# Three norms ahead instead of two: where the rows for the second product's norms are loaded

## The chip, the cores and the metric

The kernel runs on one core of one Trainium2 chip. The metric is device time in microseconds (us) of one execution; of several executions the median is taken.

## The reference

Four sublayers in a row over `x` of 2048 x 512 float32; each adds its result to its input. Sublayers 0 and 2 are a Fourier mixing, 1 and 3 a gated feed-forward (F = 1792):

```python
def _A_ref(x, ...):                      # layers 0 and 2
    a = einsum("bsd,ed->bse", x, dft_hid_re)
    b = einsum("bsd,ed->bse", x, dft_hid_im)
    return einsum("ts,bse->bte", dft_seq_re, a) - einsum("ts,bse->bte", dft_seq_im, b)

def _B_ref(x, w_gate, w_up, w_down):     # layers 1 and 3
    return (gelu(x @ w_gate) * (x @ w_up)) @ w_down

x = x + _A_ref(layernorm(x), ...)
x = x + _B_ref(layernorm(x), ...)
x = x + _A_ref(layernorm(x), ...)
x = x + _B_ref(layernorm(x), ...)
```

## The kernel before

Each float32 operand is split into a high part (a rounded copy, made on ACT, line 151) and a low part (the rest, made on DVE, line 153), and each product of two tiles is three matmuls (high x high, high x low, low x high: lines 208, 209, 210, the helper `mm3`). The large products are computed by a Strassen-like scheme with seven block products, named A11, A12, S1 to S4 and A22. A matmul writes one of eight PSUM banks (`p`); ACT copies banks out (line 195, `copied`), seeds one bank from another (line 202, `seed`) and computes the GELU (line 1019, `activated`); DVE adds (line 188, `plus`).

SBUF holds 98 slots of 128 x 512 (`s`). The free ones stand in a list: `get` takes the first one and `put` adds at the end, so the k-th tile that is taken reuses the slot that was given back earliest. In some stages two wide tiles (`wide`, `xwide`) are lent out as further slots.

The feed-forward layers handle the 2048 rows in two halves, `w` = 0 and 1, each of two blocks of 512 rows. A half takes 14 steps, `up(n)`. Step n has seven products of six matmuls each over weight tiles `wb` (loaded two steps ahead by `piece_load`, line 1009, on SP's queue), and beside them six matmuls of the product with the third weight (tiles `wc`, line 327). `first(n)` starts the bank `chain[n]` with A11 and seeds a second bank from it; `second(n)` adds A12 there and applies the GELU; `u[n]` is the copy of `chain[n]` after S2, and S3 is added to the same bank afterwards.

The rows of a half are normalised before it starts. `block_steps(layer, w)` makes eight steps `norm(i)` for this, each over 128 rows. A step takes its rows in a mixed order, by `x_load_mixed` (line 245: four transfers of 32 rows each on SP's queue), then computes mean and variance on ACT (lines 564 and 566, with a power on POOL, lines 567 and 568), applies them on ACT (line 590), transposes on DVE (line 672) into a wide tile, and after four steps POOL stores that tile (line 675). What `norm(i)` loads is the subject here: the first step loads several rows at once, a later one a row that a later step uses.

For `w` = 0 the eight steps stand among the products of the mixing layer before, in the stages of its second and third output block (`chores_at`). There the first four read output block 0 and the last four output block 1, and rows are never loaded across that border: `end` is the end of the four. For `w` = 1 they stand in the list `slow` and are run one by one, every ninth product, while half 0 is computed. Steps 0 to 3 of half 1 read output block 2 and steps 4 to 7 (rows 12 to 15 of the sixteen) block 3, which the mixing layer writes at its very end (line 278, `x_out`).

The program is written in this order, but a scheduler then places each instruction on its engine by its own estimate of times. Each engine carries out its instructions strictly in the order in which they were placed: one that waits holds all behind it. That holds for SP's queue of transfers too.

Of the kernel before, what the change touches and what calls it, by code (L numbers as in the profile page):

```python
# [21 lines left out]
NT = TB // P  # L22
# [25 lines left out]
def fnet_geglu(ctx: ExitStack, tc: tile.TileContext, x_in, ws, wh, wgu, wdn, wdc, out):  # L48
# [113 lines left out]
    def split_slot(src):  # L162
        hi, lo = sb.get(F32R), sb.get(F32R)
        split(src, hi, lo)
        return hi, lo
# [16 lines left out]
    def minus(out, a, b):  # L182
        with behind("DVE"):
            nc.vector.tensor_tensor(out, a, b, op=ALU.subtract)  # L184
# [54 lines left out]
    def x_load_mixed(layer, i):  # L239

        g, n = divmod(i, NT)
        t = sb.get()
        for j in range(NT):
            r0 = j * P + n * 32
            nc.sync.dma_start(t[j * 32:(j + 1) * 32], xs[layer, g][r0:r0 + 32])
        return t
# [335 lines left out]
    def normed(layer, i, mixed=False):  # L582
        x = row_of(layer, i, mixed)
        z = sb.get()
        rstd, shift = known.pop((layer, i), None) or norm_terms(layer, i, x, z)
        if layer == 0 and i == 0:
            for h in half:
                nc.scalar.activation(z[:, h], x[:, h], AF.Identity, bias=shift, scale=rstd)
        else:
            nc.scalar.activation(z, x, AF.Identity, bias=shift, scale=rstd)  # L590
        sb.put(x)
        return z
# [61 lines left out]
    def block_steps(layer, w):  # L654

        zt, t, wide = {}, {}, {}
        turned = [dram.tile([P, NT * D], F32, name=f"t{layer}_{w}_{part}") for part in range(2)]

        def norm(i):

            def run():
                r0 = w * 2 * NT
                end = 2 * NT if w else i // NT * NT + NT
                for k in range(i if i == 0 or i + NT == end and not w else i + 2, min(i + 3, end)):
                    fresh["mixed", r0 + k] = x_load_mixed(layer, r0 + k)
                z = normed(layer, r0 + i, True)
                part, n = divmod(i, NT)
                if n == 0:
                    assert not sb.out("z")
                    wide[part] = tpool.tile([P, NT * D], F32, name="wide")  # L670
                to = wide[part].rearrange("p (b n t) -> p b n t", n=NT, t=32)
                nc.vector.transpose(to[:, :, n], z.rearrange("p (b t) -> p b t", t=32))
                sb.put(z)
                if n == NT - 1:
                    nc.gpsimd.dma_start(turned[part], wide.pop(part))
            return run

        def fetch(c):

            def run():  # L680
                for part in range(2):
                    v = zt[c, part] = sb.get()
                    for i in range(P // 32):
                        cols = turned[part][:, (c * 4 + i) * P:(c * 4 + i + 1) * P]
                        to = v[i * 32:(i + 1) * 32]
                        (nc.gpsimd if w == 0 else nc.sync).dma_start(
                            to.rearrange("p (j t) -> p j t", t=P), cols.rearrange("(j p) t -> p j t", p=32)
                        )
            return run

        def difference(a, b):
            v = sb.get()
            minus(v, a, b)
            return v

        def first(c):
            def run():
                v = t[f"B{1 + c // 2}1", c % 2] = zt.pop((c, 0))
                blocks[f"B{1 + c // 2}1", c % 2] = split_slot(v)
            return run  # L700

        def second(c):
            def run():
                v = zt.pop((c, 1))
                if c < 2:
                    t["B12", c] = v
                    t["T1", c] = difference(v, t["B11", c])
                    sb.put(t.pop(("B11", c)))
                else:
                    c0 = c - 2  # L710
                    t["T2", c0] = difference(v, t["T1", c0])
                    t["T3", c0] = difference(v, t["B12", c0])
                    sb.put(t.pop(("B12", c0)))
                    blocks["B22", c0] = split_slot(v)
                    sb.put(v)
            return run

        def fourth(c):
            def run():
                t["T4", c] = difference(t["B21", c], t["T2", c])  # L720
                sb.put(t.pop(("B21", c)))
            return run

        def divide(name, c):
            def run():
                blocks[name, c] = split_slot(t[name, c])
                sb.put(t.pop((name, c)))
            return run

        one = [norm(i) for i in range(2 * NT)]  # L730
        two = [fetch(c) for c in range(ND)] + [first(c) for c in range(ND)] + [second(c) for c in range(ND)]
        two += [fourth(c) for c in range(2)]
        two += [divide(name, c) for name in ("T2", "T3", "T1", "T4") for c in range(2)]
        return one, two
# [773 lines left out]
```

## Time and profile before

| what | value |
|---|---|
| time, median of 3 runs | 1611.77 us (1610.68 to 1614.64) |
| time of the profiled execution | 1611.43 us |
| span of the profiled execution, first to last instruction | 1609.7 us |
| mean granted TensorE clock | 0.998 |
| TensorE (PE) busy | 1597.4 us, 99% of the span |
| VectorE (DVE), ScalarE (ACT), GpSimd (POOL) busy | 70%, 55%, 17% |
| data moved | 419.14 MB, 260 GB/s on average |

In the rows of the profile `PE` is the matmul, `PEld` the weight load beside it, `SPq` the queue on which SP issues transfers. A group `p<-s,s` writes a bank from two slots. `[6.47 <-DMA s<-x]` behind a row says that the engine stood idle for 6.47 us before it, and what ended that. Times in a timeline are us from the start of the span. The profiled execution took 1.7 us more than its span.

### The profile page before, as it was taken

To read this page: it belongs to the slowest core of one execution; us is meant where nothing else is said; L and a number is where in the kernel's file an instruction comes from. 1 tells how busy PE (TensorE), PEld (TensorE's weight loads), DVE (VectorE), ACT (ScalarE), POOL (GpSimd) and SP (SyncE) were. 2 spreads that over 40 slices of the span, in tenths; PEclk is the share of its full clock that TensorE was granted. 3 is DMA by queue.
4 is the path that set the end of the run, shared out by engine and by line. 5 is a ranking of instruction groups with operands and counts; after the bars stand their busy time and mean duration, and the time that the engine had idled before them with its cause. 6 is when DMAs were issued, how large, how long until landed. Compare 5 with 4: busy or idle time off the path is not lost.

```text
span 1609.7 us, 22615 instructions
## 1 busy us (share of the span) xinstructions
PE 1597.4 (99%) x7008; PEld 1316.5 (82%) x7008; DVE 1132.5 (70%) x1958; ACT 885.1 (55%) x1711; POOL 271.7 (17%) x469
## 2 busy tenths in 40 slices
PE   9999999999999999999999999999998999999998
PEld 6888888888888888888788888888887888888887
DVE  7997878787699783456879877777744457744574
ACT  8955466654767554546566636465444545433460
POOL 4112121242556101000040001101310000000001
PEclk9999999999999999999999999999999999999999
DMA  9878887996999899755896776878999576895445
GB/s 358 294 262 301 297 312 258 344 323 207 338 350 317 275 357 289 230 170 181 273 306 200 250 256 219 305 235 291 251 312 266 165 216 193 309 307 166 125 150 157
DMA packets 238872, 419.14 MB, mean 260 GB/s; under 512 B 28512, under 2 KB 66656, under 8 KB 237728
## 3 DMA queue, kind: packets, MB, share of 16 engines
q1 hardware_dynamic: 214512, 336.16, 65.3%
q0 software_dynamic: 24240, 81.55, 14.3%
q8 instruction: 55, 0.90, 0.2%
q14 instruction: 65, 0.53, 0.1%
HBM read 341.31 MB, written 76.28 MB: 259 GB/s over the span
## 4 chain that ended last, share of the span: by engine, by line
PE 94%; DMA 3%; DVE 1%; ACT 1%; issue 0%; SPq 0%; POOL 0%; DVEq 0%; ACTq 0%; POOLq 0%
PE p L208 31%; PE p L209 31%; PE p L210 31%; DMA s<-x 1%; DMA xwide<-x 1%; DMA s<-wc 1%; PE p L809 1%; DMA begun<-wide 0%; DVE s L153 0%; DMA s<-wb 0%; DVE s L184 0%; DMA s<-begun 0%; DVE s L188 0%; ACT s L151 0%; SPq L1271 0%
## 5 line engine op out<-in xcount | busy, mean ns | idle before, releaser
L209 PE MATMUL p<-s,s 128*128 128x512 f32 x2320 | 900.4, 390 | 0.0
L210 PE MATMUL p<-s,s 128*128 128x512 f32 x2320 | 893.7, 389 | 0.0
L208 PE MATMUL p<-s,s 128*128 128x512 f32 x2320 | 867.2, 390 | 5.9 <-ACT s L1019 4.4
L153 DVE TENSOR_TENSOR s<-s,s 128x512 fp32r<-128x512 f32 (+1 forms) x809 | 507.6, 661 | 126.7 <-ACT s L151 110.4
L151 ACT ACTIVATE s<-s 128x512 fp32r<-128x512 f32 (+1 forms) x809 | 454.5, 607 | 239.2 <-DVE s L184 65.9
L208 PEld LDWEIGHTS p<-s,s 128*128 128x128 f32 x2320 | 436.0, 188 | 98.7 <-ACT s L1019 4.9
L209 PEld LDWEIGHTS p<-s,s 128*128 128x128 f32 x2320 | 436.1, 188 | 91.2 <-DVE s L153 1.0
L210 PEld LDWEIGHTS p<-s,s 128*128 128x128 f32 x2320 | 436.2, 188 | 90.7
L188 DVE TENSOR_TENSOR s<-s,p 128x512 f32<-128x512 f32 x188 | 127.2, 683 | 166.8 <-PE p L210 136.9
L184 DVE TENSOR_TENSOR s<-s,s 128x512 f32<-128x512 f32 (+1 forms) x374 | 222.8, 612 | 5.6 <-PE p L209 3.6
L195 ACT ACTIVATE s<-p 128x512 f32<-128x512 f32 x232 | 134.6, 594 | 123.2 <-PE p L210 119.7
L1019 ACT ACTIVATE s<-s 128x512 f32<-128x512 f32 x84 | 52.8, 629 | 60.2 <-DVE s L188 50.5
L567 POOL TENSOR_SCALAR rstd<-rstd 128x1 f32<-128x1 f32 x40 | 20.5, 512 | 363.3 <-ACT s L566 347.4
L153 DVE TENSOR_TENSOR s<-xwide,s 128x512 fp32r<-128x512 f32 x71 | 47.7, 678 | 33.5 <-ACT s L151 33.2
L313 POOL DMA_DIRECT2D wb<-s x84 | 46.6, 569 | 87.8 <-ACT s L151 67.6
L1033 DVE TENSOR_TENSOR s<-s,p 128x512 f32<-128x512 f32 x56 | 38.3, 684 | 32.3 <-PE p L210 29.6
L151 ACT ACTIVATE s<-xwide 128x512 fp32r<-128x512 f32 x71 | 43.0, 621 | 15.5 <-DVE xwide L184 6.6
L1019 ACT ACTIVATE s<-p 128x512 f32<-128x512 f32 x28 | 16.7, 597 | 63.3 <-PE p L210 59.8
L590 ACT ACTIVATE s<-s,shift,rstd 128x512 f32<-128x512 f32 x56 | 44.9, 811 | 10.9 <-DMA s<-x 4.9
L202 ACT ACTIVATE p<-p 128x512 f32<-128x512 f32 x56 | 32.8, 586 | 30.6 <-PE p L210 30.4
L191 DVE TENSOR_TENSOR s<-s,s 128x512 f32<-128x512 f32 (+1 forms) x68 | 40.6, 605 | 8.6 <-DMA s<-ws 6.7
L564 ACT ACTIVATE s<-s 128x512 f32<-128x512 f32 x33 | 20.7, 626 | 46.4 <-DMA s<-x 27.9
(100 smaller groups left out, 613.4 us busy)
## 6 DMA issues: line engine op xcount, KB each, us to landing
s<-ws SPq DMA_DIRECT2D x384, 256.0 KB, 4.9
s<-wb SPq DMA_DIRECT2D x294, 256.0 KB, 5.0
s<-wc SPq DMA_DIRECT2D x182, 256.0 KB, 4.4
s<-wh SPq DMA_DIRECT2D x116, 256.0 KB, 5.1
wb<-s POOLq DMA_DIRECT2D x98, 256.0 KB, 5.4
s<-x SPq DMA_DIRECT2D x59, 256.0 KB, 5.3
xwide<-ws SPq DMA_DIRECT2D x50, 256.0 KB, 4.6
wc<-s POOLq DMA_DIRECT2D x49, 256.0 KB, 5.6
```

Source lines behind the costliest of these rows:

```text
L151: newest["ACT"] = nc.scalar.activation(hi, src, AF.Copy)
L153: newest["DVE"] = nc.vector.tensor_tensor(lo, src, f32(hi), op=ALU.subtract)
L184: nc.vector.tensor_tensor(out, a, b, op=ALU.subtract)
L188: bank_read["DVE"] = nc.vector.tensor_tensor(out, a, b, op=ALU.add)
L191: nc.vector.tensor_tensor(out, a, b, op=ALU.add)
L195: bank_read["ACT"] = nc.scalar.activation(v, src, AF.Copy)
L208: nc.tensor.matmul(ps, ah, bh, start=start, stop=False, skip_group_check=True)
L209: nc.tensor.matmul(ps, ah, bl, start=False, stop=False, skip_group_check=True)
L210: nc.tensor.matmul(ps, al, bh, start=False, stop=stop, skip_group_check=True)
L313: nc.gpsimd.dma_start(a, f32(t))
L590: nc.scalar.activation(z, x, AF.Identity, bias=shift, scale=rstd)
L1019: nc.scalar.activation(t, g, AF.Gelu_apprx_tanh)
```

## The change

In `norm(i)` the range of rows to load moves by one. Before, step 0 loads the rows of steps 0, 1 and 2, and step i the row of step i + 2. After, step 0 loads those of steps 0 to 3, and step i the row of step i + 3. For `w` = 0 this means that all four rows of a block are loaded in the first of its four steps. The number of loads and every computation stay the same; one slot more is held between the earlier load and its former place.

```diff
             def run():
                 r0 = w * 2 * NT
                 end = 2 * NT if w else i // NT * NT + NT
-                for k in range(i if i == 0 or i + NT == end and not w else i + 2, min(i + 3, end)):
+                for k in range(i if i == 0 or i + NT == end and not w else i + 3, min(i + 4, end)):
                     fresh["mixed", r0 + k] = x_load_mixed(layer, r0 + k)
                 z = normed(layer, r0 + i, True)
```

## The prediction

> **What bounds the kernel now.** I read the page first, then the waits of PE, then the stages around each of them.
>
> ```profile
> span 1609.7 us, 22615 instructions
> ...
> PE 1597.4 (99%) x7008; PEld 1316.5 (82%) x7008; DVE 1132.5 (70%) x1958; ACT 885.1 (55%) x1711; POOL 271.7 (17%) x469
> ```
>
> PE is the bound, at 99%. A load can only pay where PE stands still. The waits of PE alone:
>
> ```profile
> PE p L208 <- ACT s L1019: 4.4, 1, 4.4
> PE p L1418 <- POOL ident masks.py:199: 1.4, 1, 1.4
> PE p L208 <- DMA s<-wc: 1.1, 1, 1.1
> PE p L208 <- ACT s L195: 0.3, 1, 0.3
> ```
>
> That is the whole list. One wait is large, and it happens once. The timeline of PE shows its place, early in layer 3, half 0 (step n = 2 of 14):
>
> ```profile
> 1219.82 0.39 PE L208 MATMUL p<-s,s 128*128 128x512 f32 x1
> 1220.05 0.39 PE L209 MATMUL p<-s,s 128*128 128x512 f32 x1
> 1220.27 0.61 PE L210 MATMUL p<-s,s 128*128 128x512 f32 x2
> 1225.32 0.80 PE L208 MATMUL p<-s,s 128*128 128x512 f32 x1 [4.44 <-ACT s L1019]
> 1225.91 0.63 PE L209 MATMUL p<-s,s 128*128 128x512 f32 x1
> ...
> 1229.75 0.63 PE L209 MATMUL p<-s,s 128*128 128x512 f32 x1
> 1230.18 0.54 PE L210 MATMUL p<-s,s 128*128 128x512 f32 x1
> 1230.56 0.39 PE L208 MATMUL p<-s,s 128*128 128x512 f32 x1
> ```
>
> Ahead of the stop a matmul starts every 0.227 us (1219.82, 1220.05, 1220.27). Behind it one starts every 0.43 us (1229.75, 1230.18). The granted clock tells why:
>
> ```profile
> 763.00:768.00 5.00, 3.88 (x18) 2.90 (x17) 5.00 (x10) 2.88 (x6) 0.00 (x0) 1.00 1.05 390
> 1220.50:1225.30 4.80, 0.39 (x2) 0.00 (x0) 0.71 (x1) 2.51 (x7) 0.05 (x1) 0.83 1.02 245
> 1225.30:1230.50 5.20, 5.18 (x12) 4.16 (x13) 1.53 (x3) 4.27 (x9) 1.30 (x3) 0.50 1.02 370
> ```
>
> The third column from the end is the clock: 0.50 for 5.2 us after this stop, 1.00 around the shorter one near 766 us. The whole price: 13 starts from 1220.50 (the second of the pair of 1220.27) to 1230.56 take 10.06 us, and at 0.227 us they would take 2.95. **This place costs 7.1 us**, 0.44% of the time.
>
> What held PE is told by ACT, SP and the chain of waits, in this order:
>
> ```profile
> 1216.02 0.29 ACT L569 ACTIVATE shift<-mean,rstd 128x1 f32<-128x1 f32 x1 [0.24 <-POOL rstd L568]
> 1222.79 0.63 ACT L564 ACTIVATE s<-s 128x512 f32<-128x512 f32 x1 [6.47 <-DMA s<-x]
> ...
> 1223.42 0.80 ACT L590 ACTIVATE s<-s,shift,rstd 128x512 f32<-128x512 f32 x1
> 1224.12 0.57 ACT L195 ACTIVATE s<-p 128x512 f32<-128x512 f32 x1
> ...
> 1224.69 0.58 ACT L1019 ACTIVATE s<-p 128x512 f32<-128x512 f32 x1
> ```
>
> ```profile
> 1204.77 1.22 SPq L327 DMA_DIRECT2D s<-wc  x1
> 1206.83 2.58 SPq L1258 DMA_DIRECT2D xwide<-x  x4
> 1209.51 3.54 SPq L1009 DMA_DIRECT2D s<-wb  x3
> 1213.14 4.10 SPq L245 DMA_DIRECT2D s<-x  x4
> ...
> 1221.98 1.35 SPq L245 DMA_DIRECT2D s<-x  x3
> 1223.42 1.64 SPq L1009 DMA_DIRECT2D s<-wb  x2
> ```
>
> ```profile
> 1216.94 5.39 DMA s<-x
> 1222.46 0.32 issue
> ```
>
> The fifth norm of half 1 (step 4, row 12) stands on ACT at L564 and waits 6.47 us for its row. Its four transfers were issued from 1213.14 on, and the last one, issued at 1216.94, landed 5.39 us later, at 1222.33. Behind L564 in ACT's order stand the GELU of a bank (L1019 at 1224.69) and a copy of another (L195). PE needs the GELU's bank for its next product. So the wait is for just such a load as the change moves, and the engine that it reaches is the bound.
>
> **The change part by part.** The built programs show what the scheduler makes of it. PE's order differs in about 155 of 6986 instructions, in a few short stretches, each around norms. Three things matter.
>
> *The norm in layer 3.* On ACT, L564 of step 4 moves back by four places. Before it now stand both GELUs (the one that PE waited for, and one more) and the copy of chain[0]. Directly behind it stands the copy u[2] (L195). PE's order up to there is unchanged: the six matmuls of first(3), which stopped at 1225.32 before, and then S3, which overwrites the bank that u[2] copies. So first(3) no longer waits: its bank was complete at about 1216.8 (18 matmuls ahead of 1220.50, plus 0.39), and ACT, idle from about 1219 by the same durations as above, has read it. PE then runs 6 x 0.227 = 1.36 us more, from 1220.73 to 1222.09, and stops at S3 until u[2] is copied.
>
> When that is depends on when the row lands. On SP the load is no longer one piece behind all transposed loads (`xwide<-x`). Two of its transfers stand ahead of those and the last one behind them. Counted from the same `wb` load, the last transfer has the four `xwide` and the same `wb` loads ahead of it as before, but the `wc` load (the row at 1204.77) now comes behind it. The queues are full there (a DMA share of 1.02), so what counts is bytes: one load of 262144 bytes at 245 to 370 GB/s (the rows above) is 0.7 to 1.1 us. I take 1.1, the nearer in time: the row lands at 1221.2. L564 started 0.46 us after the landing and the next instruction 0.63 us later; the copy lasts 0.57, and PE starts 0.06 after it (1224.69 + 0.57 against 1225.32). So S3 starts at 1221.2 + 1.72 = 1222.9, **a stop of 0.8 us**. With the row no earlier than before it would be 2.0, with a row that lands before 1220.4 none.
>
> Behind it ACT owes the splits for the next `wc` product, behind L565, L566 and L569 of the same norm. By the durations above I get 0.4 us of further stops, an estimate between 0 and 0.8. Sum: 7.1 - 0.8 - 0.4 = **5.9 us saved**, between 7.1 - 2.0 - 0.8 = 4.3 and 7.1. This counts no half clock behind a short stop. The row for that is the one near 766 us:
>
> ```profile
> 767.18 0.50 PE L208 MATMUL p<-s,s 128*128 128x512 f32 x1 [1.12 <-DMA s<-wc]
> ```
>
> It kept 1.00 after 1.12 us of idling; 4.44 us did not. A stop of 0.8 us lies below both, one of 2.0 us between them.
>
> The Trainium skill ("TensorE: Matmul & The Clock Gate", "What's actually happening") says that the array falls to half clock after an idle window of about 3.4 us which runs freely. By it the stop of 2.0 us would cost no clock either, so the lower end of 4.3 us would stand; both rows agree with it.
>
> *The rows themselves.* The 32 rows keep their 128 transfers.
>
> ```profile
> L245 SPq DMA_DIRECT2D s<-x x112: 302/416/1516, 194.5 to 1257.5; - x112
> L245 SPq DMA_DIRECT2D xwide<-x x16: 324/372/1120, 266.0 to 1061.3; - x16
> ```
>
> A row is four issues of 0.416 us, 1.7 us on SP, which now stands ahead of loads that it followed. In layer 3, rows 13 to 15 come on SP right behind row 12, ahead of `wb` loads: 12 x 0.416 = 5.0 us. What hides it: `wb` is loaded two steps ahead, a step is 48 matmuls or 10.9 us, and these loads land some 5 us after their issue (the two at 1223.42 are for step 5, which starts after 1250). I take 0; with that cover gone it is up to 5.0.
>
> *Layer 1's start.* There PE also has no cover. Rows of PE, ACT, POOL and SP, in this order:
>
> ```profile
> 405.60 0.50 PE L208 MATMUL p<-s,s 128*128 128x512 f32 x1 [0.31 <-ACT s L195]
> 400.02 0.29 ACT L569 ACTIVATE shift<-mean,rstd 128x1 f32<-128x1 f32 x1 [4.95 <-POOL rstd L568]
> 393.79 5.56 POOL L567 TENSOR_SCALAR rstd<-rstd 128x1 f32<-128x1 f32 x1
> 387.07 5.51 SPq L245 DMA_DIRECT2D s<-x  x12
> 398.29 2.51 SPq L245 DMA_DIRECT2D s<-x  x4
> ```
>
> The copies that PE waits for stand behind a norm that waits for POOL, whose op took 5.56 us, and that norm's row is in the first transfers of 387.07, which stay where they are. The fourth row (398.29) moves up behind the twelve. Nothing in ACT's order changes up to 405.6. I take 0; the bounds are a gain of 0.3 (PE's idle) and a loss of 2.5 (the four issues, all of it passed on to PE).
>
> Elsewhere (the norms in layers 0 and 2) PE's list above has no wait, so nothing can be gained; the loads come no later than before. As slots are taken in the order in which they were given back, and the count of takings is equal again behind the moved load, later loads reuse the same givings-back as before. One slot less in between delays a load by one giving-back; I take 0.
>
> **Sum.** The profiled execution took 1611.43 us, 0.34 below the median of 1611.77; 1611.43 - 5.9 = 1605.5, and on the median's scale **1605.9 us**, -0.37%. About 0.3% (4.8 us) is what a measurement of this kernel can tell from no change.
>
> **The rivals.**
>
> *The wait is handed on.* The row lands no earlier, or later, since its last transfer now stands behind a `wb` load that waits for a slot from PE (the 3.54 us of 1209.51). From a landing of about 1224 on, the stop at S3 exceeds 3.6 us, and the clock may fall again (12 starts x 0.2 = 2.4 us more). Then 7.1 - 3.6 - 0.4 - 2.4 = 0.7 us is saved: 1611.1 us. For it: the full queues. Against it: one load less ahead. Chance 0.16.
>
> *The gain is given back.* Queues stay full after 1225 (share 1.02), and PE, 5.9 us earlier, meets its loads. Then the end stays: 1611.8 us. Against it: two steps of cover. Chance 0.08.
>
> *Slower: the loads become the bound.* Place: SP's queue from 1221 on. If `wb` loads land less than 5.0 us ahead of their products, removing the stop gives nothing, the twelve earlier row transfers cost 5.0 us, and such a stop halves the clock for another 2.4: 1611.8 + 7.4 = 1619.2 us. It decides from the point at which those 21.8 us of two steps, less the landing, shrink below 5. For it: the share of 1.02 and DMAs that wait for one another. Against it: PE had no such wait in the whole profile. The chance, 0.15, holds what I have not seen in the places where norms moved.
>
> That the change does nothing is excluded: in the built program the loads have moved.
>
> **How the numbers follow.** The forecast with its range of 4.3 to 7.1 us saved (1604.7 to 1607.5) has 0.61; 0.05 of that lies under 4.8 us. So faster 0.56; same 0.05 + 0.16 + 0.08 = 0.29; slower 0.15. The range reaches from 1604.4, the full 7.1 us with the 0.3 of layer 1, to the case given back, 1611.8, and leaves out the slower one.
>
> **What would show it.** Right: PE's wait for L1019 near 1220 is gone, a wait of about 0.8 us for L195 (u[2]) stands in its place, the clock stays at 1.00, ACT's wait at L564 of that norm is near 2 us instead of 6.47, and all other waits of PE are as before. Wrong: a new row of over 2 us in PE's waits, a clock of 0.50 behind 1222, or loads of `wb` as PE's releaser.

## The result: 0.25% faster, and the large stop halved instead of gone

| kernel | median, us | runs | lowest to highest |
|---|---|---|---|
| before | 1612.2 | 10 | 1610.38 to 1614.64 |
| three norms ahead | 1608.01 | 10 | 1606.56 to 1610.15 |

The ratio is 0.9975, with a 95% interval of 0.9967 to 0.9984. The change gains 4.2 us by the medians: a real gain, though under the 0.3% that the prediction named as the bound. The forecast was 1605.9 us, 5.9 us saved; 4.2 us lie just below the 4.3 to 7.1 us of the forecast, and inside the wider range, which reached to the case of no gain.

The profiled execution took 1607.73 us, 3.70 less than that of before. Its page begins like this:

```profile
span 1606.0 us, 22616 instructions
...
PE 1596.6 (99%) x7008; PEld 1316.2 (82%) x7008; DVE 1133.2 (71%) x1958; ACT 884.5 (55%) x1711; POOL 275.3 (17%) x469
```

PE is still the bound. The waits of PE after the change (us in total, times, longest):

```profile
PE p L208 <- ACT s L195: 2.3, 1, 2.3
PE p L1418 <- POOL ident masks.py:199: 1.4, 1, 1.4
PE p L208 <- DMA s<-wc: 1.3, 2, 0.8
```

The 4.4 us for the GELU (L1019) are gone. In their place stand 2.3 us for a copy (L195). The timeline of PE shows it at the same place:

```profile
1220.59 0.39 PE L209 MATMUL p<-s,s 128*128 128x512 f32 x1
1220.82 0.39 PE L210 MATMUL p<-s,s 128*128 128x512 f32 x1
1223.51 0.50 PE L208 MATMUL p<-s,s 128*128 128x512 f32 x1 [2.31 <-ACT s L195]
1223.85 0.40 PE L209 MATMUL p<-s,s 128*128 128x512 f32 x1
...
1224.55 0.47 PE L209 MATMUL p<-s,s 128*128 128x512 f32 x1
1224.81 0.63 PE L210 MATMUL p<-s,s 128*128 128x512 f32 x1
1225.24 0.63 PE L208 MATMUL p<-s,s 128*128 128x512 f32 x1
```

The six matmuls that stopped at 1225.32 before now run through, as forecast, and PE stops at S3. The next start should be 0.23 us after 1220.82; it comes at 1223.51, so PE stands still for 2.5 us. At first the matmuls start every 0.23 to 0.24 us again. From 1224.81 on they start every 0.43 us (1224.81, 1225.24): the half clock comes here too. By the clock records of the trace it begins at 1224.72, 1.2 us after PE has resumed, and lasts 3.41 us. The windows (the third column from the end is the granted clock, then DMA share and GB/s):

```profile
1215.00:1220.00 5.00, 5.00 (x24) 4.14 (x23) 2.57 (x5) 2.50 (x6) 1.31 (x2) 1.00 1.15 208
1220.50:1223.50 3.00, 0.70 (x4) 0.24 (x2) 0.00 (x0) 1.25 (x4) 0.00 (x0) 1.00 1.02 379
1223.50:1229.00 5.50, 5.49 (x17) 4.31 (x18) 2.76 (x5) 4.09 (x10) 0.74 (x2) 0.69 0.98 228
1229.00:1232.00 3.00, 3.00 (x15) 2.49 (x14) 1.13 (x2) 0.86 (x2) 0.00 (x0) 1.00 1.05 282
```

On ACT and on SP:

```profile
1217.17 0.57 ACT L1019 ACTIVATE s<-p 128x512 f32<-128x512 f32 x1
1222.25 0.63 ACT L564 ACTIVATE s<-s 128x512 f32<-128x512 f32 x1 [4.51 <-issue]
...
1222.88 0.58 ACT L195 ACTIVATE s<-p 128x512 f32<-128x512 f32 x1
```

```profile
1204.48 0.98 SPq L245 DMA_DIRECT2D s<-x  x2
1205.83 0.32 SPq L1258 DMA_DIRECT2D xwide<-x  x1
1206.50 0.82 SPq L1009 DMA_DIRECT2D s<-wb  x1
1207.98 0.32 SPq L1258 DMA_DIRECT2D xwide<-x  x1
1208.78 0.34 SPq L1009 DMA_DIRECT2D s<-wb  x1
1210.10 0.31 SPq L245 DMA_DIRECT2D s<-x  x1
1211.23 0.81 SPq L1009 DMA_DIRECT2D s<-wb  x2
1212.10 1.41 SPq L1258 DMA_DIRECT2D xwide<-x  x2
1214.30 0.31 SPq L245 DMA_DIRECT2D s<-x  x1
```

The GELU now stands ahead of the norm on ACT, the copy behind it. ACT still waits 4.51 us at L564. The profile names no transfer as the releaser, but the trace's semaphore events show the row's last transfer (issued at 1214.30) landing at 1222.18, just ahead of L564. Before it landed at 1222.33. **The row's last transfer was issued 2.6 us earlier and landed 0.15 us earlier.**

Where the 3.70 us are, counted from the starts of the matmuls (the time of a section less 0.2267 us for each matmul in it):

| section of the span, us | lost before | lost after |
|---|---|---|
| 1200 to 1250 (the stop) | 7.13 | 4.21 |
| the start, 405, 640 and 765 together | 7.4 | 6.4 |
| 1340 to 1400 (a wait for `wc` of 0.53) | 0.0 | 0.9 |
| behind the last matmul | 5.2 | 4.7 |

The stop gives 2.9 us. The rest is small, of both signs, and differs by as much between two executions of the same kernel (below, e7).

### The profile page after: what moved, and what is told of

It reads as the page before. It is cut to its first block, busy times and chain, and to the rows that moved or that the text cites. A ratio compares the mean times of both kernels' runs of the same rounds, so it can differ in the third digit from the quotient of the medians.

```text
span 1606.0 us, 22616 instructions
## 1 busy us (share of the span) xinstructions
PE 1596.6 (99%) x7008; PEld 1316.2 (82%) x7008; DVE 1133.2 (71%) x1958; ACT 884.5 (55%) x1711; POOL 275.3 (17%) x469
## 2 busy tenths in 40 slices
DMA packets 238872, 419.14 MB, mean 261 GB/s; under 512 B 28512, under 2 KB 66656, under 8 KB 237728
## 5 line engine op out<-in xcount | busy, mean ns | idle before, releaser
L195 ACT ACTIVATE s<-p 128x512 f32<-128x512 f32 x232 | 134.2, 594 | 129.7 <-PE p L210 125.9
L567 POOL TENSOR_SCALAR rstd<-rstd 128x1 f32<-128x1 f32 x40 | 24.9, 623 | 367.1 <-ACT s L566 352.2
L1019 ACT ACTIVATE s<-s 128x512 f32<-128x512 f32 x84 | 52.8, 629 | 57.9 <-DVE s L188 48.2
L1019 ACT ACTIVATE s<-p 128x512 f32<-128x512 f32 x28 | 16.7, 597 | 67.1 <-PE p L210 65.2
L564 ACT ACTIVATE s<-s 128x512 f32<-128x512 f32 x33 | 20.7, 627 | 36.9 <-PE p L209 15.6
```

Source lines behind the costliest of these rows:

```text
L195: bank_read["ACT"] = nc.scalar.activation(v, src, AF.Copy)
L1019: nc.scalar.activation(t, g, AF.Gelu_apprx_tanh)
```

## The experiments

**Theory.** Only the stop near 1220 us counts, in half 1 of layer 3. Two things make it: the place of norm step 4 on ACT, and the landing of its row. The change corrected the first in part and the second not at all, because the transposed loads (`xwide<-x`) and `wb` loads still stood ahead of the row's last transfer in a full queue. **Rivals.** The gain comes from norms elsewhere. Or the remaining stop is a matter of depth, and loading still earlier removes it. Or the queue as a whole is too full, and it doesn't matter what stands where.

Time before in these comparisons: 1612.24 us (15 runs) for the first four, 1611.02 (10 runs) for the rest.

### e1_half1_layer3 and e2_all_but_that: which place counts

Three ahead only for half 1 of layer 3, and three ahead everywhere but there. With `d` short for the depth, both edits have this form:

```diff
-                for k in range(... else i + 2, min(i + 3, end)):
+                for k in range(... else i + d, min(i + d + 1, end)):
 # e1: d = (3 if layer == 3 and w else 2)      e2: d = (2 if layer == 3 and w else 3)
```

> Three ahead for half 1 of layer 3 alone, two ahead elsewhere. My theory: the change works at one place, the stop of PE near 1220 us in layer 3, so this part alone brings nearly all of it: 3 to 4 us below the kernel before (0.9975 to 0.998), with a stop of about 2.5 us for the copy u[2] there, as in the changed kernel. Rival 1 (the gain comes from many small places where norms moved, in layers 0 to 2): within 1 us of the kernel before. Rival 2 (the small gains at 405 and 765 us, 0.6 us together, belong to the change): this kernel is 0.6 us slower than the changed one.

> The complement: three ahead everywhere but in half 1 of layer 3. My theory: PE's wait of 4.4 us for the GELU (L1019) near 1220 us is back with the half clock behind it, and the time is within 1 us of the kernel before (ratio 1.000). Rival 1 (many small places): 3 to 4 us faster.

e1: 1606.98 us, ratio 0.9967 (0.9954 to 0.9979). e2: 1609.97 us, 0.9987 (0.9978 to 0.9996). The largest wait of PE in e1, then in e2:

```profile
PE p L208 <- ACT s L195: 2.4, 2, 2.0
```

```profile
PE p L208 <- ACT s L1019: 3.0, 1, 3.0
```

The change in this half alone gives the whole gain (5.3 us by the medians, where 3 to 4 were expected; the intervals of e1 and of the whole change overlap) and has the same new wait, for the copy. Without it the old wait for the GELU is back. But e2 was 2.3 us faster than before by the medians, where about nothing was expected. In its profile the old stop was shorter: PE lost 4.9 us there against 7.1, the row landed at 1220.77 instead of 1222.33, and the half clock lasted 3.41 us instead of 6.83. Why the row landed earlier was not settled, so a small gain from norms elsewhere is not excluded.

### e3_after_turned_behind: the row's landing, on the changed kernel

The transposed loads of half 0 in layer 3 are issued behind the last transfer of row 12. ACT's order stays that of the changed kernel. (In this kernel, e4 and e8 two lines are added: L565 is L564 of before, L1020 is L1019, L1260 is L1258.)

```diff
-            nc.sync.dma_start(t[j * 32:(j + 1) * 32], xs[layer, g][r0:r0 + 32])
+            moved = nc.sync.dma_start(t[j * 32:(j + 1) * 32], xs[layer, g][r0:r0 + 32])
+        mixed_load[layer, i] = moved
...
-            rows_moved(layer, part, lambda v, outside: nc.sync.dma_start(v, outside))
+            with tc.issue_after(mixed_load[3, 12].ins) if layer == 3 and w == 0 and part == 0 else ExitStack():
+                rows_moved(layer, part, lambda v, outside: nc.sync.dma_start(v, outside))
```

> The changed kernel with one more thing: in layer 3, half 0, the transposed loads (load_turned(0)) are issued on SP behind the row of step 4; ACT's order stays. The theory now: the row landed late since its last transfer had four transposed loads ahead of it, which take 1.2 to 1.9 us each in the queues. Then it lands some 5 us earlier, near 1217, ACT is not held, and neither the stop of 2.3 us for u[2] nor the half clock behind it is left: 4.2 us below the changed kernel, 1603.5 to 1604.5, ratio 0.9948 to 0.9955. Rival (bytes in the queue ahead, as the prediction reckoned, so that 1 MB less is worth 3 to 4 us but the row waits for the wb loads and PE anyway): a stop of over 1 us stays, 1606 to 1607.

1602.89 us, ratio 0.9938 (0.9924 to 0.9952). SP, ACT and the windows of the profile:

```profile
1210.08 1.01 SPq L1010 DMA_DIRECT2D s<-wb  x2
1211.73 0.32 SPq L245 DMA_DIRECT2D s<-x  x1
1212.10 0.94 SPq L1260 DMA_DIRECT2D xwide<-x  x2
```

```profile
1217.45 0.58 ACT L1020 ACTIVATE s<-p 128x512 f32<-128x512 f32 x1
1217.93 0.62 ACT L565 ACTIVATE s<-s 128x512 f32<-128x512 f32 x1
...
1218.54 0.58 ACT L195 ACTIVATE s<-p 128x512 f32<-128x512 f32 x1
```

```profile
1220.00:1223.00 3.00, 3.00 (x15) 2.49 (x14) 1.71 (x3) 2.64 (x6) 0.74 (x2) 1.00 1.04 306
```

The row's last transfer, issued at 1211.73 with no transposed load ahead, landed at 1215.31, after 3.6 us instead of the 7.9 of the changed kernel. L565 waits for nothing, the copy comes at 1218.54 instead of 1222.88, and PE does not stop: it lost nothing between 1200 and 1250. The time is a little below the expected one.

### e4_before_turned_behind: the landing alone

The same edit on the kernel before.

> The kernel before (two ahead) with the transposed loads of layer 3, half 0, issued behind the row of step 4; ACT's order stays that of before, with the norm ahead of the GELU. The theory: what counts is when the row lands, not how many steps ahead it is loaded; it lands near 1217 instead of 1222.3, L564 starts then, the GELU is done before PE needs it at 1220.7, and all 7 us are saved: 1604.5 to 1605.5, ratio 0.995 to 0.9955, faster than the changed kernel. Rival (the place on ACT decides, and the row's landing only follows the fullness of the queues): a stop of over 2 us at the same place stays, 1608 or more.

1605.67 us, ratio 0.9954 (0.9941 to 0.9966): the ratio as expected, the time 0.2 us above the expected range. The row landed at 1215.58. On ACT the norm still stands ahead of copy and GELU, as before, and it does no harm now:

```profile
1217.80 0.63 ACT L565 ACTIVATE s<-s 128x512 f32<-128x512 f32 x1
1219.14 0.58 ACT L195 ACTIVATE s<-p 128x512 f32<-128x512 f32 x1
1219.71 0.58 ACT L1020 ACTIVATE s<-p 128x512 f32<-128x512 f32 x1
```

PE lost nothing there. The profiled execution of e4 had another stop elsewhere, 1.16 us at 275 us in the first layer, in code that is the same as before:

```profile
275.33 0.98 PE L208 MATMUL p<-s,s 128*128 128x512 f32 x3 [1.16 <-ACT s L151]
```

### e5_before_norm_later: the place on ACT alone

The kernel before, with no load touched. The instructions of step 4 are placed behind the newest splits.

```diff
             norms, others = block_steps(layer, 1)
+            if layer == 3:
+                norms[4] = paced(norms[4])
```

> The kernel before, loads untouched; in layer 3 norm step 4 of half 1 is placed on ACT behind the newest splits in program order, so that both GELUs, the copy u[2] and more now stand ahead of it. The theory (an engine in order: PE stops only since the norm that waits for its row stands ahead of ACT work that PE needs): the row lands at about 1222 as before, ACT has passed its bank work by then, PE does not stop near 1220: 5 to 7 us below the kernel before, ratio 0.9955 to 0.997. Rival (the full queues hold PE too, through the wb or wc loads): a wait of PE for a DMA of over 1 us takes the stop's place.

1604.26 us, ratio 0.9958 (0.9944 to 0.9971), as expected. The row landed at 1222.19, as late as before. The norm reads it only here:

```profile
1250.70 0.62 ACT L564 ACTIVATE s<-s 128x512 f32<-128x512 f32 x1
```

All waits of PE in this run:

```profile
PE p L1420 <- POOL ident masks.py:199: 1.4, 1, 1.4
PE p L208 <- DMA s<-wc: 1.0, 1, 1.0
PE p L208 <- ACT s L195: 0.3, 1, 0.3
PE p L208 <- ACT s L151: 0.2, 1, 0.2
```

The stop is gone, as in e3 and e4, though the row lands no earlier. So no load has to move. The stop needed both: a row that lands late, and an ACT instruction that reads it ahead of work for PE. Taking away either one is enough.

### e6_four_ahead: the depth

```diff
-                for k in range(... else i + 2, min(i + 3, end)):
+                for k in range(... else i + 4, min(i + 4 + 1, end)):
```

> Four ahead instead of three, everywhere. If loading earlier were what helps, this should be no worse than the changed kernel (1608). The theory of the queue says otherwise: on SP the transfers of two rows (steps 4 and 5) now alternate, the row of step 4 is complete only behind five wb loads and two transposed loads, and on ACT its norm stands ahead of one GELU and of u[2]; PE stops when that GELU's bank is wanted, for 1 to 4 us, with the half clock from 2 us on: 1607 to 1612, not faster than the changed kernel.

1606.03 us, ratio 0.9968 (0.9955 to 0.9981). The time came out below what was expected; the interval overlaps that of the changed kernel, so a gain of the fourth step is not shown. Two of the waits of PE:

```profile
PE p L208 <- ACT s L195: 1.1, 1, 1.1
PE p L208 <- ACT s L1019: 0.9, 1, 0.9
```

The first is at 406.84 us, at the start of layer 1. The second is the stop, at 1223.74 us: it is there again, shorter, and for the GELU. ACT and the windows there:

```profile
1222.48 0.63 ACT L564 ACTIVATE s<-s 128x512 f32<-128x512 f32 x1 [3.16 <-issue]
1223.11 0.58 ACT L1019 ACTIVATE s<-p 128x512 f32<-128x512 f32 x1
```

```profile
1222.00:1223.50 1.50, 0.85 (x4) 0.38 (x2) 0.69 (x1) 1.02 (x3) 0.00 (x0) 1.00 1.18 182
1223.50:1228.00 4.50, 4.16 (x17) 3.13 (x18) 0.46 (x1) 4.24 (x13) 1.49 (x4) 1.00 1.02 237
```

The row is complete at about 1222.4, no earlier than with depth two or three: loaded another norm ahead, it still shares the queue with the transposed loads. The stop, 1.06 us by the starts of the matmuls, cost no clock. PE lost 1.65 us in all between 1200 and 1250. In this profile it lost more than in the others at two places ahead: 1.4 us near 405 (0.4 to 0.6 in the others) and 1.2 near 640 (up to 0.5).

### e7_before_again: how far one execution stands for the kernel

A second profile of the kernel before.

> The kernel before once more, for a second profiled execution. If the stop near 1220 us hangs on when the row lands in full queues, it differs from one execution to the next: 3 to 5 us idle (4.6 in the first one, 3.2 in the kernel with three ahead everywhere else), each with the half clock. If it is fixed by the order of instructions: 4.6 again within 0.3.

1610.22 us (one run). The same stop stands at the same place:

```profile
1224.29 0.80 PE L208 MATMUL p<-s,s 128*128 128x512 f32 x1 [4.66 <-ACT s L1019]
```

ACT waited 6.69 us for the row. The stop is no accident of one execution, and its length agrees with the second of the two expectations, a stop fixed by the order of the instructions. PE lost 6.5 us there against 7.1 in the first profile. The small waits differ more: 0.9 us instead of 1.4 near 765, 6.0 instead of 5.2 behind the last matmul. Differences under about 1 us between two profiles are not explained here for that reason.

### e8_turned_once: is a full queue the cause?

e3, with a second call of the transposed load left out. In three half-layers this call loads the same rows again; without it the first copy is the one that is read.

```diff
         elif pairs == NP:
-            load_turned(0)
+            pass
```

> The changed kernel with the transposed loads behind the row (as in the experiment before) and with the second of two identical load_turned(0) calls left out, in layers 1 and 3 (the rows are loaded twice into the wide tile, and only the second is read). If the queues still cost PE time (the waits for wc near 765 us and 1362 us, about 1 us together), this gives up to 1 us: 1601.9 to 1602.9. If not, 1602.9 as without it.

1602.59 us, ratio 0.9947 (0.9935 to 0.9960), against 0.9938 (0.9924 to 0.9952) for e3. The data moved fell from 419.14 to 416.00 MB:

```profile
DMA packets 232536, 416.00 MB, mean 260 GB/s; under 512 B 28320, under 2 KB 60320, under 8 KB 231392
```

No difference to e3 is shown, so less traffic gives nothing beyond e3. As e3 has no stop left at this place, e8 can't say what traffic is worth there; that the order counts is shown by e3 and e4, which move the same bytes as the kernels that they start from. e3 and e8 are the fastest versions, about 0.5 to 0.6% below the kernel before.

## Why the prediction was right and where it was not

**What bounds the kernel, and the place: right.** e1 puts the gain in that half of layer 3, and e4 and e5 show both halves of the stated cause: the row's landing and the place of L564 on ACT.

**The order on ACT: right, and it is what the change gained.** first(3) no longer waits. The landing moved by only 0.15 us, so nearly all of the 2.9 us there come from the four places on ACT. From landing to S3 it took 1.33 us (1222.18 to 1223.51), 0.4 less than the 1.72 forecast.

**The landing ("one load fewer ahead", 1221.2 us): wrong.** This is the first term that was mis-sized: the landing of 1222.18 instead of 1221.2 costs 1.0 us. The count was right. SP's rows go back to the same `wc` load in both kernels, before and then after:

```profile
1196.31 0.32 SPq L327 DMA_DIRECT2D s<-wc  x1
1197.35 7.22 SPq L1009 DMA_DIRECT2D s<-wb  x10
```

```profile
1194.88 0.39 SPq L327 DMA_DIRECT2D s<-wc  x1
1195.54 8.13 SPq L1009 DMA_DIRECT2D s<-wb  x9
```

From there to the row's last transfer SP issues thirteen `wb` loads, four transposed loads and the row's four transfers in both, and a further `wc` load only before. The price of that load was about right too. Take the last `wb` load that has the same loads ahead of it in both kernels (issued at 1203.72 before and 1203.35 after). By the semaphore events, from its landing to the row's it was 12.22 us before (1210.11 to 1222.33) and 11.01 us after (1211.17 to 1222.18): 1.2 us less, with 1.1 forecast. But the queue was already 1.06 us later at that `wb` load, though it was issued 0.4 us earlier, and that used up the saving. The prediction took the queue's time up to there as unchanged. In the profiles of the changed kernel, e1 and e3 this load landed at 1211.2 to 1211.7, in those of before, e2, e4, e5 and e7 at 1209.2 to 1210.9. Why it is later is not shown.

What cost most stood ahead in both kernels. From the same `wb` load to the row it was 3.64 us in e3 (1211.67 to 1215.31) and 5.12 us in e4 (1210.46 to 1215.58), 7.4 and 7.1 us less than with the four transposed loads in between. That is about 1.8 us for each of them, an estimate from these four profiles, beside 1.2 us for the `wc` load of the same 262144 bytes. Bytes alone don't give the time in the queue.

**When PE arrives: not reckoned.** The prediction let PE reach S3 at 1222.09, as late as before. Small gains at four earlier places brought it there at 1221.05, while the row landed only 0.15 us earlier. Being 1.0 us earlier at a transfer that is not earlier makes the stop 1.0 us longer. The second profile of before (e7) also had PE there 1.26 us earlier than the first (and its row 1.03 us earlier), so this term is in part the chance of one execution. So the stop of 0.8 became 0.8 + 1.0 + 1.0 - 0.4 = 2.4 us; measured are 2.5.

**"No half clock behind a short stop": wrong.** This is the second term. It was reckoned at 0 for 0.8 us, and also for the 2.0 us of the lower end. In the changed kernel it is 4.21 - 2.47 = 1.7 us, half of the 3.41 us for which the clock was low. The 0.4 us of further stops did not show. On the 5.9 us forecast that makes 5.9 - 1.7 (the longer stop) - 1.7 (the clock) + 0.4 = 2.9, which is what was measured at this place.

**The total: in part luck.** 2.9 us lie below the 4.3 us that the prediction gave as its lower end. That end was made of a stop of 2.0 us and 0.8 us of further stops, without a half clock; measured were a stop of 2.5 us, the half clock and no further stops. The total of 4.2 us comes near it only through a further 1.3 us (0.8 in the two profiles), in small waits which differ by such amounts between two profiles of the kernel before. The interval of the ratio, 2.6 to 5.3 us, holds 2.9 as well.

**Rows earlier on SP at no cost, and the rival of the `wb` loads: as forecast.** PE's list names no `wb` load. One small wait for `wc` is new (0.53 us at 1363), within what differs from execution to execution.

**The rivals.** "The wait is handed on" holds in its first half: the row landed hardly earlier (0.15 us), and the clock fell. Its point of decision, a stop of 3.6 us, was set too high, so the truth lies between it and the forecast. Nothing was given back behind 1225: e3 to e5 keep what they gain at the stop to the end.

## What to carry to other kernels

An in-order engine that feeds the bound engine should never have an instruction with a late operand ahead of a copy or an activation that the bound engine is waiting for; moving that instruction back (e5) needs no change to any load. When a transfer is late, count what stands ahead of it in the queue in the new order, look at what kinds of loads these are, and ask when the queue gets there, before trusting an earlier issue: here 2.6 us of earlier issue gave 0.15, and taking four transposed loads out of the way gave 6.9. And reckon the time at which the bound engine arrives anew, because every gain ahead of a fixed transfer lengthens the stop in front of it.

## What the hardware did that was not expected

The clock fell after shorter stops than was thought. Idle stops of PE and the clock behind them, each from the matmul starts of one profile:

| idle, us | kernel | clock behind it |
|---|---|---|
| 1.06 | e6 | 1.00 |
| 1.28 | before, near 766 | 1.00 |
| 1.32 | e4, near 274 | 1.00 |
| 2.18 | e1 | falls to half |
| 2.47 | three ahead | falls to half |
| 3.21 | e2 | falls to half |
| 4.6 and 4.82 | before, e7 | falls to half |

```profile
1223.30:1228.00 4.70, 4.69 (x14) 3.70 (x15) 1.96 (x4) 3.35 (x8) 0.74 (x2) 0.64 0.91 237
```

This is the window behind the stop of e1, with a clock of 0.64. In the table the clock fell after stops of 2.18 us and more, and not after stops of 1.32 us and less.

The clock records of the trace tell more. In each of the five profiles in which the clock fell at this stop, it fell 1218.56 us after its first rise near the start of the kernel, although the stops began at different times, 1213.8 to 1215.8 us after that rise. It stayed low for 3.41 us, in the first profile of before for twice that, and 1218.56 us is 357 times 3.413 us. In these runs the clock is therefore set at the ends of windows of 3.41 us that run on from its first rise, and what counts is how long PE stands still within one of them: it fell at the end of windows with 2.18 us (e1) to 3.41 us (e7) of idling, and not at the end of the one with 1.38 us, in which e7's long stop began. A low window in which PE is busy throughout costs half of its 3.41 us, 1.7 us.

By this a stop of 2.47 us that lies half in one window and half in the next would have cost no clock, an estimate from the 1.38 us. Where the windows lie differs from execution to execution: the first rise came 4.70 to 6.36 us after the start of the span in the ten profiles. So the half clock behind a stop of this length is in part luck. One of the ten executions of the changed kernel (1607.02 us) has a mean granted clock of 1.000, where one low window would leave 0.999.

The Trainium skill ("TensorE: Matmul & The Clock Gate", "What's actually happening") gives an idle window of about 3.4 us that runs freely. The traces agree on the length and on the free running. They differ in that the window need not be idle throughout: 2.18 us of idling in it were enough. No run here varied the stop by itself.
